# Down products in rounds of three F tiles in a fused attention and GEGLU kernel

## The chip, the cores and the metric

The kernel runs on one core of a Trainium2 chip. The metric is the device time of one execution in microseconds (us); lower is better. TensorE (PE) does the matrix products, VectorE (DVE), ScalarE (ACT) and GpSimd (POOL) the elementwise work, SyncE (SP) issues the DMAs.

## The reference, cut to what matters

Sequence S = 2048, model width D = 576, hidden width F = 4608, H = 32 heads of DH = 18, all in fp32.

```python
def A_ref(x, wqkv, wo):                                   # attention
    q, k, v = split_heads(x @ wqkv)                       # each [H, S, 18]
    p = softmax(einsum("bhqd,bhkd->bhqk", q, k) * 18 ** -0.5)
    return merge_heads(einsum("bhqk,bhkd->bhqd", p, v)) @ wo

def B_ref(x, w_gate, w_up, w_down):                       # GEGLU
    return (gelu(x @ w_gate) * (x @ w_up)) @ w_down

xn = layernorm(x)
return x + A_ref(xn, wqkv, wo) * silu(B_ref(xn, w_gate, w_up, w_down))
```

## The kernel before

**Number format.** Products run on fp32r operands. A factor is split into a high part and a low part, and a product of two factors is made of three matrix products (high·high, high·low, low·high) that accumulate in one PSUM bank. The cut costs two GpSimd instructions a tile (L94 for the high part, L95 for the low part). The names follow it: `wh`, `wl` for gate and up weights, `dh`, `dl` for w_down, `hh`, `hl` for the activated hidden values.

**Prologue (lines 138 to 349).** Layernorm, transpositions and the projections to q, k and v. The split operands of the attention (`qk`, `vs`), the normalised x (`xhs`) and wo go to DRAM and come back by DMA when wanted.

**Sections.** After it the feed-forward part and the attention are interleaved. Tokens are worked in 4 blocks of 512 (`NB`); F is cut into 36 tiles of 128. One *section* works one F tile of one block, so there are 144. In a section TensorE does 27 *pairs* of gate and up products (L369; each pair fills the two halves of the PE rows) into the banks `pg` and `pu`. The first 9 sections (`FIRST`) are the lead, the next 128 carry the attention, the last 7 are the epilogue. The 128 are 32 units (4 heads x 512 queries) of 4 sections (`NA`). In each of them `spread` puts 16 score products (`pe`, L684) and 16 products for the row maxima of a unit to come (`pm`, L653) between the pairs. ScalarE makes the exponentials of `pe` (L685 into `pT`), VectorE the maxima of `pm` (L654).

**End of a section.** What comes behind the pairs stands in this order in the program: the *value block*, 32 products of probabilities and values into `acc` (L718, in column tiles of 32); once in a unit `max_neg` and `max_end` (a transposition of the maxima on TensorE, L667); the `tasks` (output groups, below); `downs` (the down products); and `finish`, in which GpSimd cuts the activated tile `t1` into `hh` and `hl`. The activation itself (`activate`, L382 to L390) runs over ScalarE and VectorE while the next section begins: Square (ScalarE), L383 (VectorE, reads `pg`), a copy of `pg` to `t2` (ScalarE, L386), L387 (VectorE, reads `pu`), Tanh (ScalarE, L388), L390 (VectorE, reads t1 and t2). When a unit ends, ScalarE copies its accumulator to `accs` (L723), a DMA stores that to DRAM (`oT`), and `sums` and `reciprocals` bring the softmax denominators back as `rT`.

**Down products.** Two F tiles (`G` = 2) make a *round*; a block has 18 rounds (`NR`). For a round, `down` makes 8 accumulation groups (4 token tiles x 2 column halves of 288): in each, 3 products a tile, 6 in all (L406), into one of two banks `py` (tag "s", which the scores use as well). VectorE evicts each group into Y, by a copy in the round r == 0 of a block (L410), by an addition otherwise (L412). Within the attention a run has all 8 groups, 48 products, and stands in every second section; around the borders of the attention, and in the last round but one of a block, it is halved into 24 and 24 over two sections:

```python
once = n in ATT and n + G in ATT and r != NR - 2
FF["down"].append((b, r, FF["hs"], wd, FF["Y"], (2 * h, 2 * h + 1), n + 1 + (0 if once else h)))
```

The w_down rows of a round come in one DMA into a tile [128, 2, 576] of the raw buffers (two of them, shared with the raw gate and up weights, which come in as two loads a section and are cut in three pieces of 128x384 each). `hh` and `hl` have 3 buffers each, `dh` and `dl` one.

**Output groups.** When the attention of a block is done, `load_o` brings its sums from DRAM with the reciprocal denominators `den`, `norm_o` multiplies and cuts them on GpSimd (L506), and `project_o` multiplies by wo: 8 groups a block, 15 products each (L550), one in every second section; the group also combines with the gated feed-forward of that block. `gates` (L432) makes the silu of finished Y on ScalarE and GpSimd and stores it. `at(n, part, ...)` files these steps under an attention section.

**Order.** Only TensorE runs in the order that is written in the program; for the other engines a scheduler orders the instructions by their dependencies, save those that are wrapped in `keep_in_program_order`.

**Buffers that the change touches.** VS (values) has 3 buffers (`VB`), `load_v(n + 2)` stands ahead of the value block of section n. KS has 7. `m2` (the negated maxima) has 2, `accs` one of its own, `t2` one.

Of the kernel before, what the change touches and what calls it, by code (L numbers as in the profile page):

```python
# [32 lines left out]
SLOTS = 8  # L33
NA = NS // SLOTS
VC = NT // NA
KB, VB = 7, 3
LEAD = NS + SLOTS
G = 2
NR = F // (G * P)
NF = NB * NR * G  # L40
FIRST = (0, 0, 5, 5, 6, 6, 6, 6, 6)
ATT = range(len(FIRST), len(FIRST) + NU * NA)
MROW = 3 * DH
HO = 7
KO = HO * DH
# [22 lines left out]
def kernel(ctx: ExitStack, tc: tile.TileContext, x, wqkv, wo, w_gate, w_up, w_down, out):  # L68
# [17 lines left out]
    ident = const.tile([P, P], F32, name="ident")  # L86
    make_identity(nc, ident)
    identr = const.tile([P, P], F32R, name="identr")
    nc.gpsimd.tensor_copy(identr, ident)
    all_t = slice(0, TB)  # L90


# [43 lines left out]


    with tc.tile_pool(name="pro", bufs=1) as pro, tc.tile_pool(name="pps", bufs=1, space=PSUM) as pps:

        def load_rest(c0, n):  # L140

# [237 lines left out]
    def activate(pg, pu, early):  # L379

        t1 = ffn.tile([P, TB], F32, name="t1", bufs=1)
        nc.scalar.activation(t1, pg, AF.Square)  # L382
        nc.vector.scalar_tensor_tensor(t1, t1, 1.0 / GC, pg, op0=ALU.add, op1=ALU.mult)  # L383
        if early:
            t2 = ffn.tile([P, TB], F32, name="t2", bufs=1)
            nc.scalar.activation(t2, pg, AF.Copy)  # L386
            nc.vector.tensor_tensor(t2, t2, pu, op=ALU.mult)  # L387
        nc.scalar.activation(t1, t1, AF.Tanh, scale=GC * GS)  # L388
        if early:
            nc.vector.scalar_tensor_tensor(t1, t1, 1.0, t2, op0=ALU.add, op1=ALU.mult)  # L390
        else:
            nc.vector.scalar_tensor_tensor(t1, t1, 1.0, pg, op0=ALU.add, op1=ALU.mult)
            nc.vector.tensor_tensor(t1, t1, pu, op=ALU.mult)
        return t1

    def down(b, r, hs, wd, Y, js):
        for j in js:
            tt = slice(j * P, (j + 1) * P)
            for c in range(2):
                cc = slice(288 * c, 288 * c + 288)  # L400
                py = ps.tile([P, 288], F32, name="py", tag="s", bufs=2)
                n = 0
                for g in range(G):
                    hh, hl = hs[g]
                    for a, w in ((hh, wd[0]), (hh, wd[1]), (hl, wd[0])):
                        nc.tensor.matmul(py, a[:, tt], w[:, g, cc], start=(n == 0), stop=(n == 3 * G - 1))  # L406
                        n += 1
                yy = Y[:, j, cc]
                if r == 0:
                    nc.vector.tensor_copy(yy, py)  # L410
                else:
                    nc.vector.tensor_tensor(yy, py, yy, op=ALU.add)  # L412
                if b == NB - 1 and r == NR - 1:
                    finals.append((Y, j, c))
        if b < NB - 1 and r == NR - 1:
            FF["gates"] += [(b, j, c, Y) for j in js for c in range(2)]

    def gates():
# [17 lines left out]
    def section(specials=(), tag="f", raw_d=None, early=None):  # L436

        n = FF["n"]
        FF["n"] += 1
        b, r = divmod(n // G, NR)  # L440
        g = n % G
# [4 lines left out]
        nxt = load_gu((n + 1) % (NR * G), keep) if n + 1 < NF else None  # L446
        if nxt:
            for k in range(NG - 1):
                split_gu(nxt, k)
        if g == G - 1:  # L450
            raw = FF["rawd"] = raw_d() if raw_d else raw_tile([P, G, D])
            nc.sync.dma_start(raw, w_down[r * G * P:(r + 1) * G * P, :].rearrange("(g p) n -> p g n", p=P))
            if early:
                FF["wd"] = early(raw)
        for p in spread(pairs, specials):
            p()
        if nxt:
            split_gu(nxt, NG - 1)
        FF["w"] = nxt
        if n + 1 < NF and (n + 1) % (NR * G) == 0:  # L460
            FF["xd"] = load_xd(b + 1)
        FF["act"] = activate(pg, pu, n < ATT.stop)

# [6 lines left out]
    def finish(pool=ffn, cut=split, bufs=1):  # L470

        n = FF["n"] - 1
        b, r = divmod(n // G, NR)
        hh = ffn.tile([P, TB], F32R, name="hh", bufs=G + 1)
        hl = ffn.tile([P, TB], F32R, name="hl", bufs=G + 1)
        cut(hh, hl, FF["act"])
        FF["hs"].append((hh, hl))
        if n % G == G - 1:
            wd = FF.pop("wd", None)
            if not wd:  # L480
                wd = [pool.tile([P, G, D], F32R, name=m, bufs=bufs) for m in ("dh", "dl")]
                cut(*wd, FF["rawd"])
            for h in range(2):
                once = n in ATT and n + G in ATT and r != NR - 2
                FF["down"].append((b, r, FF["hs"], wd, FF["Y"], (2 * h, 2 * h + 1), n + 1 + (0 if once else h)))


    op = ctx.enter_context(tc.tile_pool(name="op", bufs=1, reuse_waits="tile"))
# [85 lines left out]
    for b in range(NB):  # L574
        last = b == NB - 1
        for k in range(NK):
            t0 = b * AB + max(-(-min(H, (k + 1) * HO) // QD) * NA + 3, 22 + 3 * k)
            if not (last and k == NK - 1):
                at(t0, 0, load_o, b, k)
                at(t0 + 2 - last, 2, norm_o, k)  # L580
        first = (b + 1) * AB + 1 if last else max((b + 1) * AB + 6, (b + 1) * NR * G - len(FIRST) + 3)
        if not last:
            first += (first + len(FIRST)) % G
        at(first - 2, 0, load_wo, 0)
        at(first - 1, 2, split_o, 0)
        for i in range(GROUPS):
            n = first + i * (1 if last else G)
            if last and n >= ENDS - 1:
                continue
            if not last:  # L590
                at(n, 0, load_xy, b, i)
                at(n + 1, 0, store_y, b, i)
            at(n, 1, lambda b=b, i=i: project_o(b, i, S2[0]))
            if i == TB // P - 1:
                at(n + 1, 0, load_wo, 1)
            if i + 1 < GROUPS:
                at(n, 2, split_o, i + 1)


    with tc.tile_pool(name="att", bufs=1, reuse_waits="tile") as att:  # L600
# [55 lines left out]
        def max_neg(u):  # L656

            nm = att.tile([P, 4 * QD], F32, name="nm", bufs=1)
            nc.vector.tensor_reduce(nm, MX[u].rearrange("p a t c -> p (a t) c"), axis=AX.X, op=ALU.max, negate=True)
            m2 = NM[u] = att.tile([P, 2, 4 * QD], F32R, name="m2", bufs=2)  # L660
            nc.vector.tensor_copy(m2[:, 0], nm)
            nc.vector.tensor_tensor(m2[:, 1], nm, f(m2)[:, 0], op=ALU.subtract)

# [46 lines left out]
        def values(u, kt):  # L710
            j, g = divmod(u, NQ)
            if kt == 0:
                ACC[u] = ps.tile([P, TB], F32, name="acc", tag="acc", bufs=1)
            pt = PT.pop((u, kt))
            for a in range(QD):
                c, t = divmod(kt, VC)
                v = t * VW + (DH + 1) * a
                nc.tensor.matmul(ACC[u][32 * a:32 * a + 32, :], VS[(u * NA + c) % VB][:, v:v + 32], pt[:, a, :],  # L718
                                 start=(kt == 0), stop=(kt == NT - 1), skip_group_check=True)
            if kt == NT - 1:  # L720
                cols = slice(j * TB, (j + 1) * TB)
                acc = att.tile([P, TB], F32, name="accs")
                nc.scalar.activation(acc, ACC[u], AF.Copy)  # L723
                nc.sync.dma_start(oT[g, :, cols], acc)
                rt = rT[QD * g:QD * (g + 1), cols]
                if u < NU - 1:
                    todo.setdefault(((u + 1) * NA, 0), []).insert(0, lambda: sums(u, rt))
                    at((u + 1) * NA + 2, 2, reciprocals, u, rt)
                else:
                    at(NU * NA - 1, 2, last_sums, u, rt)  # L730
# [42 lines left out]
        for n in range(NU * NA):  # L773
# [107 lines left out]
```

## Time and profile before

| | before |
|---|---|
| median of 3 runs, us | 2657.58 |
| lowest, highest, us | 2653.82, 2659.47 |
| profiled execution, us | 2655.82 |
| its span, us | 2654.0 |
| mean granted TensorE clock | 0.999 |
| busy TensorE products / weight loads, us | 2639.6 (99%) / 2052.3 (77%) |
| busy VectorE, us | 2002.5 (75%) |
| busy ScalarE, us | 1504.2 (57%) |
| busy GpSimd, us | 1392.5 (52%) |
| DMA read / written, MB | 266.58 / 52.85 |

The span goes from the first to the last instruction that the profile records, so 1.8 us of the profiled execution lie around it. Busy times are of one profiled execution. A busy TensorE does not say that its products follow each other at the best pace: the ends of products are modelled, and a product that waits in its queue can look long. Distances between the starts of neighbouring products say more. Releasers (`<-`) name the instruction whose end set a waiting one free.

### The profile page before, as it was taken

What the parts mean: (1) busy time and instruction counts of PE and PEld (TensorE: products, weight loads), DVE (VectorE), ACT (ScalarE), POOL (GpSimd) and SP (SyncE); (2) the same over time, 40 slices, a digit from 0 to 9 for tenths busy, and PEclk for the clock granted to TensorE, in tenths of its full rate; (3) what the DMA queues carried; (4) which work ended last, traced back from release to release, by engine and by line L of the source; (5) the groups of instructions that cost most, each with busy time, mean ns of one, the idle gap of its engine ahead of it and who ended that gap; (6) DMA issues with size and microseconds to landing.
All of it is one profiled execution on the core that took longest, in us unless ns stands there. A gap on an engine that the chain in (4) does not pass through costs nothing.

```text
span 2654.0 us, 55993 instructions
## 1 busy us (share of the span) xinstructions
PE 2639.6 (99%) x21032; PEld 2052.3 (77%) x21032; DVE 2002.5 (75%) x3440; ACT 1504.2 (57%) x2690; POOL 1392.5 (52%) x1488
## 2 busy tenths in 40 slices
PE   9999999999999999999999999999999999999999
PEld 8888777777777777777777777777777777777788
DVE  5327888888887888777888887778888877788445
ACT  3222466666666666555666665556666655566632
POOL 2126544545466555555447655554446755555564
PEclk9999999999999999999999999999999999999999
DMA  8875433333345434444336434434335444444341
GB/s 257 265 240 144 115 99 101 98 101 104 98 124 133 106 100 108 121 113 124 100 109 156 117 103 105 124 96 136 104 103 122 133 115 123 107 109 122 77 110 58
DMA packets 390874, 323.66 MB, mean 122 GB/s; under 512 B 105736, under 2 KB 305928, under 8 KB 390604
## 3 DMA queue, kind: packets, MB, share of 16 engines
q1 hardware_dynamic: 390604, 320.08, 44.6%
q8 instruction: 167, 2.74, 0.5%
q14 instruction: 103, 0.84, 0.1%
HBM read 266.58 MB, written 52.85 MB: 120 GB/s over the span
## 4 chain that ended last, share of the span: by engine, by line
PE 97%; POOL 1%; DVE 1%; DMA 1%; issue 0%; ACT 0%; SPq 0%; POOLq 0%; DVEq 0%
PE pg L369 26%; PE py L406 18%; PE acc L718 17%; PE pe L684 10%; PE pm L653 9%; PE pu L369 8%; PE po L159 7%; PE po L550 2%; PE pt L221 0%; POOL wl L95 0%; DVE mx L654 0%; DMA xx<-in_A_x_dram 0%; POOL th L432 0%; PE pm L667 0%; DMA raw<-in_B_w_gate_dram 0%
## 5 line engine op out<-in xcount | busy, mean ns | idle before, releaser
L685 ACT ACTIVATE pT<-pe 128x512 f32<-128x512 f32 x2048 | 1162.8, 599 | 704.1 <-PE pm L653 476.1
L654 DVE TENSOR_REDUCE mx<-pm 128x1 f32<-128x512 f32 x2048 | 1288.5, 685 | 52.1 <-PE pm L653 28.0
L369 PE MATMUL pg<-xd,wh 64*128 64x512 f32 x2592 | 948.3, 398 | 0.5 <-issue 0.5
L369 PE MATMUL pu<-xd,wh 64*128 64x512 f32 x2592 | 948.3, 398 | 0.0
L684 PE MATMUL pe<-q,KS 56*128 56x512 f32 x2048 | 812.5, 405 | 0.0
L653 PE MATMUL pm<-KS,q 54*128 54x512 f32 x2048 | 794.6, 394 | 4.7 <-DVE mx L654 4.7
L369 PEld LDWEIGHTS pg<-xd,wh 64*128 64x128 f32 x2592 | 483.0, 187 | 66.0 <-issue 34.8
L94 POOL TENSOR_SCALAR wh<-raw 128x384 fp32r<-128x384 f32 x432 | 223.8, 519 | 547.6 <-PE pu L369 292.7
L369 PE MATMUL pg<-xd,wl 64*128 64x512 f32 x1296 | 508.2, 392 | 0.0
L369 PE MATMUL pu<-xd,wl 64*128 64x512 f32 x1296 | 507.8, 392 | 0.0
L369 PEld LDWEIGHTS pu<-xd,wh 64*128 64x128 f32 x2592 | 484.1, 187 | 7.6 <-DVE t L387 1.6
L718 PE MATMUL acc<-pT,VS 128*32 128x512 f32 x4096 | 466.0, 595 | 0.0
L95 POOL TENSOR_TENSOR wl<-raw,wh 128x384 fp32r<-128x384 f32 x432 | 442.3, 1025 | 34.3
L684 PEld LDWEIGHTS pe<-q,KS 56*128 56x128 f32 x2048 | 370.2, 184 | 81.3 <-ACT pT L685 20.2
L653 PEld LDWEIGHTS pm<-KS,q 54*128 54x128 f32 x2048 | 377.0, 185 | 29.2 <-DVE mx L654 7.6
L412 DVE TENSOR_TENSOR Y<-py,Y 128x288 f32<-128x288 f32 x544 | 248.7, 457 | 187.6 <-PE py L406 186.7
L406 PE MATMUL py<-dh,hh 128*128 128x288 f32 x1152 | 352.8, 306 | 1.4 <-DVE Y L410 1.2
L406 PE MATMUL py<-dl,hh 128*128 128x288 f32 x1152 | 339.6, 295 | 0.0
L406 PE MATMUL py<-dh,hl 128*128 128x288 f32 x1152 | 338.7, 294 | 0.0
L718 PEld LDWEIGHTS acc<-pT,VS 128*32 128x32 f32 x4096 | 120.6, 109 | 275.7 <-issue 264.4
L369 PEld LDWEIGHTS pg<-xd,wl 64*128 64x128 f32 x1296 | 242.4, 187 | 17.0
L406 PEld LDWEIGHTS py<-dh,hh 128*128 128x128 f32 x1152 | 215.8, 187 | 44.1 <-issue 37.7
(118 smaller groups left out, 2935.2 us busy)
## 6 DMA issues: line engine op xcount, KB each, us to landing
KS<-qk SPq DMA_DIRECT2D x1536, 36.0 KB
raw<-in_B_w_gate_dram SPq DMA_DIRECT2D x144, 288.0 KB
raw<-in_B_w_up_dram SPq DMA_DIRECT2D x144, 288.0 KB
raw<-in_B_w_down_dram SPq DMA_DIRECT2D x68, 576.0 KB
VS<-vs SPq DMA_DIRECT2D x128, 152.0 KB
qk<-t SPq DMA_DIRECT2D x72, 256.0 KB
q<-qk SPq DMA_DIRECT2D x384, 36.0 KB
xd<-xhs SPq DMA_DIRECT2D x24, 384.0 KB
```

The costliest lines, as they stand in the source:

```text
L94: first = nc.gpsimd.tensor_scalar(hi, raw, 1.0, 1.0, op0=ALU.mult, op1=ALU.mult)
L95: nc.gpsimd.tensor_tensor(lo, raw, f(hi), op=ALU.subtract)
L159: nc.tensor.matmul(o, st, m, start=(i == 0), stop=(i == len(TERMS) - 1))
L369: nc.tensor.matmul(o, w[1 + wp][k][rr, c, :], xd[xp][k][rr, c, :], start=(i == 0), stop=(i == len(terms) - 1))
L406: nc.tensor.matmul(py, a[:, tt], w[:, g, cc], start=(n == 0), stop=(n == 3 * G - 1))
L412: nc.vector.tensor_tensor(yy, py, yy, op=ALU.add)
L550: nc.tensor.matmul(po[:, 0:288], o[x][0:n, k, :], OW[w][0:n, k, :], start=(m == 0), stop=(m == len(terms) - 1))
L653: nc.tensor.matmul(pm, QS[u, r][rr, t * P:(t + 1) * P], KS[(u * NA + c) % KB][r][rr, :], start=True, stop=True)
L654: nc.vector.tensor_reduce(MX[u][:, 2 * r + a, t, c:c + 1], pm, axis=AX.X, op=ALU.max)
L684: nc.tensor.matmul(pe, KS[(u * NA + c) % KB][r][rr, t * P:(t + 1) * P], QS[u, r][rr, :], start=True, stop=True)
L685: nc.scalar.activation(PT[u, kt][:, 2 * r + a, :], pe, AF.Exp, scale=SCALE)
L718: nc.tensor.matmul(ACC[u][32 * a:32 * a + 32, :], VS[(u * NA + c) % VB][:, v:v + 32], pt[:, a, :], start=(kt == 0), stop=(kt == NT - 1), s ...
```

## The change

- A round has up to three F tiles (`GM` = 3). The list `ROUNDS` gives the tiles of each round, block by block: block 0 has seven rounds of two, seven of three and one of one; blocks 1 and 2 one of two, eleven of three and one of one; block 3 one of two, eight of three and five of two. `PLACE` maps a section to its block, round, place in the round, size of the round and whether the round is the block's last.
- Within the attention a round's down products stand in one section (`WHOLE`), the one behind its last tile: 8 groups of 9 products, 72, for a round of three; 48 for two; 24 for one. The rounds that are halved are those at the borders of the attention.
- For rounds of three, w_down comes per F tile, [128, 576], a section after the tile's own section (`late`), and is cut into one third of `dh` and `dl`.
- Output groups stand in sections of `WHOLE`, so every third section for the most part, and `load_o` and `norm_o` move (norm_o to one section behind load_o).
- Buffers: `hh` and `hl` keep 3 buffers for 3 tiles in use (3 for 2 before), `dh` and `dl` hold three tiles, VS has 2 and its load is issued behind the value block, `m2` has 1, `accs` shares the buffer of `t2`, and `ident` lives in the prologue's pool only.

The products of the two kernels are the same in number and shape.

```diff
-KB, VB = 7, 3
+KB, VB = 7, 2
-G = 2
-NR = F // (G * P)
-NF = NB * NR * G
+FT = F // P
+NF = NB * FT
+G, GM = 2, 3
+ROUNDS = [[2] * 7 + [3] * 7 + [1], [2] + [3] * 11 + [1], [2] + [3] * 11 + [1], [2] + [3] * 8 + [2] * 5]
+PLACE = [(b, r, g, m, r == len(ms) - 1) for b, ms in enumerate(ROUNDS) for r, m in enumerate(ms) for g in range(m)]
+WHOLE = [n + 1 for n, (b, r, g, m, _) in enumerate(PLACE) if g == m - 1 and n in ATT and n + G in ATT]
...
-            t2 = ffn.tile([P, TB], F32, name="t2", bufs=1)
+            t2 = ffn.tile([P, TB], F32, name="t2")
...
-    def down(b, r, hs, wd, Y, js):
+    def down(b, r, end, hs, wd, Y, js):
...
-                for g in range(G):
-                    hh, hl = hs[g]
+                for g, (hh, hl) in enumerate(hs):
                     for a, w in ((hh, wd[0]), (hh, wd[1]), (hl, wd[0])):
-                        nc.tensor.matmul(py, a[:, tt], w[:, g, cc], start=(n == 0), stop=(n == 3 * G - 1))
+                        nc.tensor.matmul(py, a[:, tt], w[:, g, cc], start=(n == 0), stop=(n == 3 * len(hs) - 1))
...
-        if g == G - 1:
-            raw = FF["rawd"] = raw_d() if raw_d else raw_tile([P, G, D])
-            nc.sync.dma_start(raw, w_down[r * G * P:(r + 1) * G * P, :].rearrange("(g p) n -> p g n", p=P))
+        late = n > 0 and PLACE[n - 1][3] == GM
+        if late:
+            rawd = raw_tile([P, D])
+            nc.sync.dma_start(rawd, w_down[(n - 1) % FT * P:((n - 1) % FT + 1) * P, :])
+        if m < GM and g == m - 1:
+            raw = FF["rawd"] = raw_d() if raw_d else raw_tile([P, m, D])
+            t = n % FT + 1
+            nc.sync.dma_start(raw, w_down[(t - m) * P:t * P, :].rearrange("(g p) n -> p g n", p=P))
...
         for p in spread(pairs, specials):
             p()
+        if late:
+            k = PLACE[n - 1][2]
+            if k == 0:
+                FF["wd3"] = [ffn.tile([P, GM, D], F32R, name=w) for w in ("dh", "dl")]
+            split(*(w[:, k] for w in FF["wd3"]), rawd)
+            if k == GM - 1:
+                FF["down"] = [(*e[:4], FF["wd3"], *e[5:]) if e[4] is None else e for e in FF["down"]]
...
-        hh = ffn.tile([P, TB], F32R, name="hh", bufs=G + 1)
-        hl = ffn.tile([P, TB], F32R, name="hl", bufs=G + 1)
+        hh = ffn.tile([P, TB], F32R, name="hh", bufs=GM)
+        hl = ffn.tile([P, TB], F32R, name="hl", bufs=GM)
...
-                once = n in ATT and n + G in ATT and r != NR - 2
-                FF["down"].append((b, r, FF["hs"], wd, FF["Y"], (2 * h, 2 * h + 1), n + 1 + (0 if once else h)))
+                FF["down"].append((b, r, end, FF["hs"], wd, FF["Y"], (2 * h, 2 * h + 1), n + 1 + (0 if n + 1 in WHOLE else h)))
...
-            t0 = b * AB + max(-(-min(H, (k + 1) * HO) // QD) * NA + 3, 22 + 3 * k)
+            t0 = b * AB + max(-(-min(H, (k + 1) * HO) // QD) * NA + 3, 26 - 2 * last + 2 * k)
...
-                at(t0 + 2 - last, 2, norm_o, k)
-        first = (b + 1) * AB + 1 if last else max((b + 1) * AB + 6, (b + 1) * NR * G - len(FIRST) + 3)
-        if not last:
-            first += (first + len(FIRST)) % G
+                at(t0 + 1, 2, norm_o, k)
+        places = [n - len(FIRST) for n in WHOLE if n - len(FIRST) >= (b + 1) * AB + 5]
+        first = (b + 1) * AB + 1 if last else places[0]
...
-            n = first + i * (1 if last else G)
+            n = first + i if last else places[i]
...
-            m2 = NM[u] = att.tile([P, 2, 4 * QD], F32R, name="m2", bufs=2)
+            m2 = NM[u] = att.tile([P, 2, 4 * QD], F32R, name="m2", bufs=1)
...
-                acc = att.tile([P, TB], F32, name="accs")
+                acc = ffn.tile([P, TB], F32, name="accs", tag="t2")
...
-            load_v(n + 2)
             if i == 1 and u + 2 < NU:
...
                 values(u, kt)
+            load_v(n + 2)
```

More of the change, by code (lines that the diff above doesn't have):

```diff
@@ L84 @@
     xhs = [dram.tile([2, D, TB], F32, name=f"xhs{b}") for b in range(NB)]
-    ident = const.tile([P, P], F32, name="ident")
-    make_identity(nc, ident)
     identr = const.tile([P, P], F32R, name="identr")
-    nc.gpsimd.tensor_copy(identr, ident)
     all_t = slice(0, TB)
@@ L138 @@
     with tc.tile_pool(name="pro", bufs=1) as pro, tc.tile_pool(name="pps", bufs=1, space=PSUM) as pps:
+        ident = pro.tile([P, P], F32, name="ident")
+        make_identity(nc, ident)
+        nc.gpsimd.tensor_copy(identr, ident)
         def load_rest(c0, n):
@@ L412, in down @@
                     nc.vector.tensor_tensor(yy, py, yy, op=ALU.add)
-                if b == NB - 1 and r == NR - 1:
+                if b == NB - 1 and end:
                     finals.append((Y, j, c))
-        if b < NB - 1 and r == NR - 1:
+        if b < NB - 1 and end:
             FF["gates"] += [(b, j, c, Y) for j in js for c in range(2)]
@@ L439, in section @@
         FF["n"] += 1
-        b, r = divmod(n // G, NR)
-        g = n % G
+        b, _, g, m, _ = PLACE[n]
         pairs, pg, pu = gate_up(tag)
@@ L445, in section @@
         keep = tc.keep_in_program_order if n == NU * NA + len(FIRST) + 1 else lambda i: i
-        nxt = load_gu((n + 1) % (NR * G), keep) if n + 1 < NF else None
+        nxt = load_gu((n + 1) % FT, keep) if n + 1 < NF else None
         if nxt:
@@ L459, in section @@
         FF["w"] = nxt
-        if n + 1 < NF and (n + 1) % (NR * G) == 0:
+        if n + 1 < NF and (n + 1) % FT == 0:
             FF["xd"] = load_xd(b + 1)
@@ L472, in finish @@
         n = FF["n"] - 1
-        b, r = divmod(n // G, NR)
-        hh = ffn.tile([P, TB], F32R, name="hh", bufs=G + 1)
-        hl = ffn.tile([P, TB], F32R, name="hl", bufs=G + 1)
+        b, r, g, m, end = PLACE[n]
+        hh = ffn.tile([P, TB], F32R, name="hh", bufs=GM)
+        hl = ffn.tile([P, TB], F32R, name="hl", bufs=GM)
         cut(hh, hl, FF["act"])
         FF["hs"].append((hh, hl))
-        if n % G == G - 1:
+        if g == m - 1:
             wd = FF.pop("wd", None)
-            if not wd:
-                wd = [pool.tile([P, G, D], F32R, name=m, bufs=bufs) for m in ("dh", "dl")]
-                cut(*wd, FF["rawd"])
+            if m < GM and not wd:
+                wd = [pool.tile([P, G if pool is not ffn else GM, D], F32R, name=w, bufs=bufs) for w in ("dh", "dl")]
+                cut(wd[0][:, 0:m], wd[1][:, 0:m], FF["rawd"])
             for h in range(2):
-                once = n in ATT and n + G in ATT and r != NR - 2
-                FF["down"].append((b, r, FF["hs"], wd, FF["Y"], (2 * h, 2 * h + 1), n + 1 + (0 if once else h)))
+                FF["down"].append((b, r, end, FF["hs"], wd, FF["Y"], (2 * h, 2 * h + 1), n + 1 + (0 if n + 1 in WHOLE else h)))
     op = ctx.enter_context(tc.tile_pool(name="op", bufs=1, reuse_waits="tile"))
```

## The prediction

> **What bounds the kernel now.** I read the page first, then the chain of waits in order of time, then the timeline of TensorE, VectorE, ScalarE and GpSimd across single sections.
>
> ```profile
> PE 2639.6 (99%) x21032; PEld 2052.3 (77%) x21032; DVE 2002.5 (75%) x3440; ACT 1504.2 (57%) x2690; POOL 1392.5 (52%) x1488
> ...
> PE 97%; POOL 1%; DVE 1%; DMA 1%; issue 0%; ACT 0%; SPq 0%; POOLq 0%; DVEq 0%
> ```
>
> TensorE is busy for 99% of the span and is 97% of the chain that ends last. The products do not change in number (3456 down products, 21032 in all), so the time can change only through the steps between products. The chain in order of time (start, us, what) shows what a section's end costs:
>
> ```profile
> 361.12 3.57 PE acc L718 x32
> 364.69 6.64 PE py L406 x48
> ...
> 381.71 3.57 PE acc L718 x32
> 385.28 0.43 PE pg L369
> ...
> 416.20 3.57 PE acc L718 x32
> 419.77 0.18 PE pm L667
> ...
> 1021.72 3.57 PE acc L718 x32
> 1025.29 2.18 PE po L550 x15
> 1027.47 6.42 PE py L406 x48
> ```
>
> The value block (L718) takes 3.57 whatever follows it. A run of 48 down products (L406) takes 6.64 behind it, 6.42 behind an output group (L550). A transposition of the maxima (L667) adds 0.18. The timeline shows where a run loses time:
>
> ```profile
> 364.62 0.40 PE L406 MATMUL py<-dh,hh 128*128 128x288 f32 x1
> 364.86 0.30 PE L406 MATMUL py<-dl,hh 128*128 128x288 f32 x1
> 364.99 0.29 PE L406 MATMUL py<-dh,hl 128*128 128x288 f32 x1
> ...
> 366.32 0.31 PE L406 MATMUL py<-dh,hh 128*128 128x288 f32 x1
> 366.47 0.29 PE L406 MATMUL py<-dl,hh 128*128 128x288 f32 x1
> ...
> 371.04 0.29 PE L406 MATMUL py<-dh,hl 128*128 128x288 f32 x1
> 371.26 0.50 PE L369 MATMUL pg<-xd,wh 64*128 64x512 f32 x1
> ```
>
> Averaged over all runs from such starts, one product follows the other by 0.132; 48 of them are 6.35, so 0.29 of the 6.64 is loss. Entry: the second product comes 0.237 after the first (0.24 above), 0.105 too late. Exit: the next pair comes 0.220 after the last product, 0.088 too late. The rest, 0.09, lies in the third to eighth accumulation group, where the bank is used again: the step after the group's first product is 0.15 (366.32 to 366.47), not 0.13. VectorE shows why:
>
> ```profile
> 365.72 0.46 DVE L412 TENSOR_TENSOR Y<-py,Y 128x288 f32<-128x288 f32 x1 [0.84 <-PE py L406]
> ...
> 836.05 1.13 DVE L390 SCALAR_TENSOR_TENSOR t<-t,t 128x512 f32<-128x512 f32 x1
> ```
>
> The first group's last product starts at 365.39; its eviction starts 0.33 later and takes 0.46. The next user of that bank gets going some 0.15 after that, so a bank comes back 0.94 after its group's last start. With six products a group the next user stands there after 7 x 0.132 = 0.93: just too early each time. (The second line is for a rival.)
>
> **The change part by part**, against the profiled execution's 2655.8 us (span 2654.0); the median of the runs is 2657.6, 1.8 above it.
>
> *Fewer runs.* The order of the built program has 63 runs of down products for 83: 37 of 72, 7 of 48 and 19 of 24, where there were 61 of 48 and 22 of 24. Twenty exits go: 20 x 0.088 = -1.8. Runs straight behind a value block fall from 41 to 20: 21 x 0.105 = -2.2. Behind output groups (25 both times) there is no entry loss. Sum -4.0. The page "TensorEngine Tiling (Array Packing)" of the Trainium skill (section Key Properties) says that changing the tiling mode drains TensorE. Taken as one price for every change, with the step from value block to pairs for it (0.52 for 0.10), that makes 20 x 0.42 = -8.4 here; the rows give each change its own price, and I use those.
>
> *Nine products a group.* Where a run holds three F tiles the next user of a bank stands there after 10 x 0.132 = 1.32, the bank is back after 0.94, and the 0.09 a run should vanish. 54 of the 61 runs of 48 go: 54 x 0.09 = -4.9. The other bound is that the 0.015 a group is the price of waiting at all; then only the 17 rounds that no longer exist (72 before, 55 after) save it, -1.5. I take -4.9, because the second group of each run, whose bank was free long before, shows no late step.
>
> *One-tile rounds.* Three blocks end in a round of one tile: 24 products in eight groups of three. There the bank loop of 0.94 stands against 4 x 0.132 = 0.53, so two groups take 0.94 + 2 x 0.132 = 1.21, not 0.79. Following eight groups through, the last product starts 4.39 after the first, not 3.18: +1.2 each, 3.6 in all. Bounds 0 and 5 (VectorE still busy with the activation when the run starts).
>
> *Transpositions.* 28 stand now between value block and pairs (0.18 each); 7 of these will stand before a run or output group, where the average over the three such places is 0.033: -1.0. Pairs behind a transposition alone take 10.15 on average and 10.05 otherwise (8 of 27 wait some 0.37 for L387): -0.7. 27 more sections of pairs follow a value block and not a run, at +0.01: +0.3. Sum -1.4.
>
> *Two stalls.* The first run of blocks 1 and 3 now waits 1.0 and 0.5 for the Y copy (815.8 and 2095.6), because GpSimd, held by a wait for den, cut the activation late. In the built order that GpSimd step (L506) stands a section earlier and there are two sections of cover. -1.0, bounds -1.5 and 0.
>
> *Pieces of w_down, and queues.* 111 pieces at 128x576 replace 55 splits at 128x1152 (1.16 + 2.68). One piece is half of that, 1.92, or the 0.67 + 1.43 of the row of 126x576, 2.10: up to 20 us of GpSimd, which is at 52%. The loads are 56 more issues of 0.4 on SP. Each piece shares the two raw buffers with the gate and up weights: its load waits for their third split, and their next load for its split. Placed by rows (third split from 3.3 into the section, 1.5 long; loads some 3 to 4; piece 1.9; two splits 3.1; hh and hl 1.9), the tightest split ends 15 us before its first product, since weights are cut nearly two sections ahead. Also hh has no spare buffer now: in a section with a run GpSimd waits for the run's end, with the piece and the splits behind it, and they need 5.4 of the 13.9 that the next section lasts. 0. The loads of VS with two buffers wait for the value block of the same section, and are used 24 later: 0.
>
> *ScalarE.* The accumulator's copy (L723, 0.60) takes t2's buffer, so it waits for L390. All 32 copies stand in sections with a run now; 17 will not. There L390 ends 0.26 after the next pairs start (average), the copy lasts to 0.91, and the first exponential starts at 0.92, not 0.83; its bank is wanted 0.3 after its end. 0; up to 17 x 1.0 = +17 if that cover is gone (rival 2).
>
> Sum: -4.0 - 4.9 + 3.6 - 1.4 - 1.0 = -7.7. Execution 2655.8 to 2648.1, median 2657.6 to 2649.9.
>
> **The rivals.** *1: the late step of a reused bank stays.* Then -1.5 stands for -4.9, and the sum is -4.3: 2653.3. For it: the late step has nearly one size everywhere, as a fixed price would. Against it: the loop from the rows (0.94 against 0.93) gives that size too.
>
> *2: ScalarE becomes late.* L390 reads two SBUF tiles. It takes 0.69, but 1.13 at 836.05, where GpSimd's subtraction ran beside it, and 1.53 at most; 16 of 137 are over 0.76. If the new pieces push GpSimd's third or second split under L390, it ends 0.84 later, the copy ends near 1.75, the first exponential is 0.92 late and the third score product waits 0.6. With 16 exponentials of 0.60 in 10.05 us ScalarE cannot catch up, and up to 0.4 returns at the next activation. Seventeen such copies cost 10 to 17: 2660 to 2667. Slower than before it is from 0.45 a copy. Against it: in the order GpSimd's split for the end of the pairs ends 1.8 after them and L390 starts at 3.4; only where GpSimd runs 1.6 late do they meet. The Trainium skill's page "SBUF — State Buffer" (section Who interferes with whom) states the mechanism: a VectorE instruction with two SBUF inputs contends with GpSimd instructions that read SBUF. The trace agrees (0.69 against 1.13), and also in that evictions, with one SBUF input, take 0.46 with GpSimd busy or idle.
>
> *3: every change of tiling costs alike.* With the page's rule -8.4 stands for -4.0: 2645.5. Against it are the rows of entry and exit.
>
> That the change does not do what it says is excluded by the built order (37 runs of 72).
>
> **How the numbers follow.** 0.2% is 5.3 us, about what a measurement of this kernel can tell from no change. Forecast 0.62, rival 1 0.18, rival 2 0.13, rival 3 0.07. The forecast's own range, by the bounds of the one-tile rounds and the stalls, is -10 to -5: 2647 to 2653; 0.06 of it is within 0.2%. Rival 1 (-4.3, +-1) is mostly within: 0.15, and 0.03 faster. Rival 2 gives 0.10 slower and 0.03 within. So faster 0.62 - 0.06 + 0.03 + 0.07 = 0.66, same 0.06 + 0.15 + 0.03 = 0.24, slower 0.10. The range leaves out the worse half of rival 2 and most of rival 3, and takes in run-to-run scatter of the median of 2: 2646 to 2659.
>
> **What would show it.** Right: runs of 72 in the chain at about 9.73 behind a value block (72 x 0.132 + 0.20) and 9.6 behind an output group; steps inside groups all 0.13; three runs of 24 near 4.6; no stall at the first run of a block; TensorE still 97% of the chain. Wrong: a step of 0.15 in each group of nine (rival 1); L390 often over 1.0, exponentials starting later than 1.2 after the pairs' start, waits of pe for ACT (rival 2); any wait of L369 for GpSimd's splits, or of L406 for dl, would say that the cover of the pieces was misjudged.

## The result: slower, and the profile after

| | before | changed |
|---|---|---|
| median, us | 2658.05 (4 runs) | 2674.48 (4 runs) |
| lowest, highest, us | 2653.82, 2659.47 | 2671.98, 2675.79 |
| profiled execution, its span, us | 2655.82, 2654.0 | 2671.98, 2670.2 |
| mean granted TensorE clock | 0.999 | 0.996 |

The ratio is 1.0064, 95% interval 1.0052 to 1.0076: 16 us slower where 7.7 faster was forecast. In the changed kernel the down product is L408, the pairs L372, the value block L729, norm_o's multiplication L518, the activation L385 to L393. The page's busy times and the shares of the chain:

```profile
PE 2641.6 (99%) x21032; PEld 2051.7 (77%) x21032; DVE 1958.0 (73%) x3303; ACT 1502.7 (56%) x2690; POOL 1423.6 (53%) x1602
...
PE 94%; DVE 3%; DMA 1%; POOL 1%; issue 1%; ACT 0%; SPq 0%; POOLq 0%; DVEq 0%; ACTq 0%
```

Busy TensorE moved by 2.0 us and its share of the chain fell from 97% to 94%: products wait, they do not take longer. The chain in order of time (start, us, what) shows runs as forecast, 9.73 behind a value block (forecast 9.73) and 9.51 behind an output group (9.6):

```profile
494.87 3.57 PE acc L729 x32
498.44 9.73 PE py L408 x72
...
1235.13 2.17 PE po L562 x15
1237.31 9.51 PE py L408 x72
```

Elsewhere the chain leaves TensorE. The two largest places, with the pairs at their end:

```profile
1299.97 4.88 DMA OT<-oT
...
1304.98 1.30 POOL OT L518
1306.30 4.78 DMA den<-rT
...
1312.46 0.62 POOL hh L94
...
1313.16 1.29 POOL hl L95
...
1314.47 0.60 ACT t L385
...
1317.19 0.50 PE pu L372
```

```profile
1374.19 9.28 DMA raw<-in_B_w_down_dram
...
1383.54 0.67 POOL dh L94
...
1388.83 0.59 POOL hh L94
...
1389.49 1.27 POOL hl L95
...
1390.79 0.60 ACT t L385
...
1392.88 0.76 PE pg L372
```

Read them from the end. The pairs wait for a bank that the activation has not read. Its Square (L385) waits for t1, whose last reader is the cut `hl` of the tile before. That cut stands on GpSimd behind an instruction that waits for a DMA: norm_o for OT and den in the first, a piece of w_down in the second, whose load was issued among those of q, OT and wo and took 9.28 us. TensorE stood 1.9 and 5.2 us. (Its waits put the first down to the cut `dl`, which ended at the same moment, 1316.56; the pairs do not read it. The copy of `pg`, L389, ended at 1316.42 and freed the bank.) The windows show what came on top (columns: window, length, busy PE, PEld, DVE, ACT, POOL, granted clock, DMA share, GB/s):

```profile
1387.70:1390.00 2.30, 0.00 (x0) 0.00 (x0) 0.00 (x0) 0.00 (x0) 2.13 (x4) 1.00 1.10 250
1390.00:1392.50 2.50, 0.00 (x0) 0.00 (x0) 0.69 (x1) 0.96 (x2) 2.23 (x3) 0.57 0.39 111
1393.50:1396.50 3.00, 3.00 (x15) 2.40 (x16) 2.08 (x3) 1.05 (x2) 0.15 (x1) 0.50 0.62 167
1397.50:1400.50 3.00, 3.00 (x30) 2.63 (x28) 3.00 (x6) 2.34 (x6) 2.92 (x4) 1.00 0.29 74
...
1319.00:1322.00 3.00, 3.00 (x16) 2.43 (x16) 2.15 (x5) 1.92 (x4) 0.00 (x0) 0.50 1.10 244
```

The clock is at 0.50 for 3.4 and 4.3 us of the pairs that follow: 15 or 16 products in 3 us, then 30. The pairs behind the two stalls are 2.1 and 2.2 us longer than usual, most of it by that.

By the starts of products, section by section (the usual length of each kind of section end and of the pairs times its count, and what exceeds it), the 16.2 us between the spans are:

| | us | forecast |
|---|---|---|
| section ends: fewer runs, nine products a group, transpositions before runs | -9.8 | -9.9 |
| three one-tile rounds (from the last product of the pairs to the next pairs 8.52, not 7.29) | +3.7 | +3.6 |
| usual length of the pairs, 123 full sections | +1.6 | -0.4 |
| prologue and end | -1.5 | 0 |
| stalls and late activations above that | +22.2 | -1.0 |

The stalls: GpSimd's late cuts 4.0 at 1314, 7.5 at 1387 and 3.2 at 1467, late KS loads 5.8 (1334, 1934, 2149), ScalarE 0.9 (849), the rest small.

### The profile page after: what moved, and what is told of

It is laid out like the page before. It is cut to its first block, busy times and chain, and to the rows that moved or that the text cites. A ratio compares the mean times of both kernels' runs of the same rounds, so it can differ in the third digit from the quotient of the medians.

```text
span 2670.2 us, 56169 instructions
## 1 busy us (share of the span) xinstructions
PE 2641.6 (99%) x21032; PEld 2051.7 (77%) x21032; DVE 1958.0 (73%) x3303; ACT 1502.7 (56%) x2690; POOL 1423.6 (53%) x1602
## 4 chain that ended last, share of the span: by engine, by line
PE 94%; DVE 3%; DMA 1%; POOL 1%; issue 1%; ACT 0%; SPq 0%; POOLq 0%; DVEq 0%; ACTq 0%
PE pg L372 25%; PE py L408 17%; PE acc L729 16%; PE pe L695 10%; PE pm L664 8%; PE pu L372 8%; PE po L162 7%; PE po L562 2%; DVE mx L665 1%; DMA raw<-in_B_w_down_dram 0%; PE pt L224 0%; DVE Y L414 0%; DVE t L386 0%; DVE t L390 0%; POOL wl L95 0%
## 5 line engine op out<-in xcount | busy, mean ns | idle before, releaser
L372 PE MATMUL pg<-xd,wh 64*128 64x512 f32 x2592 | 951.2, 399 | 8.1 <-ACT t L389 5.6
L372 PE MATMUL pu<-xd,wh 64*128 64x512 f32 x2592 | 950.4, 399 | 0.6 <-DVE t L390 0.5
L372 PEld LDWEIGHTS pg<-xd,wh 64*128 64x128 f32 x2592 | 484.5, 187 | 92.9 <-issue 34.1
L372 PE MATMUL pu<-xd,wl 64*128 64x512 f32 x1296 | 509.2, 393 | 0.0
L372 PE MATMUL pg<-xd,wl 64*128 64x512 f32 x1296 | 509.0, 393 | 0.0
L372 PEld LDWEIGHTS pu<-xd,wh 64*128 64x128 f32 x2592 | 485.7, 187 | 8.6 <-DVE t L390 2.9
L729 PE MATMUL acc<-pT,VS 128*32 128x512 f32 x4096 | 466.0, 595 | 0.0
L414 DVE TENSOR_TENSOR Y<-py,Y 128x288 f32<-128x288 f32 x408 | 185.3, 456 | 235.9 <-PE py L408 235.0
L408 PE MATMUL py<-dh,hh 128*128 128x288 f32 x1152 | 346.4, 301 | 4.4 <-DVE Y L412 2.7
L94 POOL TENSOR_SCALAR wh<-raw 128x384 fp32r<-128x384 f32 x432 | 233.8, 542 | 214.6 <-PE pu L372 102.9
L408 PE MATMUL py<-dh,hl 128*128 128x288 f32 x1152 | 339.8, 295 | 0.0
L408 PE MATMUL py<-dl,hh 128*128 128x288 f32 x1152 | 338.9, 294 | 0.0
L729 PEld LDWEIGHTS acc<-pT,VS 128*32 128x32 f32 x4096 | 120.2, 109 | 276.6 <-issue 261.6
L94 POOL TENSOR_SCALAR dh<-raw 128x576 fp32r<-128x576 f32 (+1 forms) x121 | 86.5, 715 | 404.1 <-DMA raw<-in_B_w_down_dram 390.8
L372 PEld LDWEIGHTS pg<-xd,wl 64*128 64x128 f32 x1296 | 242.9, 187 | 16.6
```

The source lines that it names most:

```text
L94: first = nc.gpsimd.tensor_scalar(hi, raw, 1.0, 1.0, op0=ALU.mult, op1=ALU.mult)
L372: nc.tensor.matmul(o, w[1 + wp][k][rr, c, :], xd[xp][k][rr, c, :], start=(i == 0), stop=(i == len(terms) - 1))
```

## The experiments

Each is named by what it changes; the kernel before ran on the same chip.

**Does the slowness come with the buffers, the pieces or the output part?** First the changed kernel with rounds of two only:

```diff
-ROUNDS = [[2] * 7 + [3] * 7 + [1], [2] + [3] * 11 + [1], [2] + [3] * 11 + [1], [2] + [3] * 8 + [2] * 5]
+ROUNDS = [[2] * 18] * 4
```

> The changed kernel with eighteen rounds of two F tiles in every block: no pieces of w_down, no run of 72, output groups every second section again; all the buffer changes stay (two VS buffers with the load behind the value block, one m2, the accumulator's copy in t2's buffer, no more than three hh and hl, norm_o one section behind load_o). Theory A (the pieces of w_down, through the two shared raw buffers and the in-order queues of GpSimd and SP, cause the stalls): about the time before, 2655 to 2661 us. Theory B (output groups every third section push the next block's OT loads together behind the last cut of OT, and GpSimd is held there): the same, 2655 to 2661. Theory C (the smaller buffers cause the stalls): 2666 us or more, with waits of the pairs for the activation and of the maxima for KS.

2677.95 us (ratio 1.008, 1.0065 to 1.0095). No theory had this. The time went in three places, 8.3, 7.7 and 6.6 us over the usual length of the pairs, each where a block begins: TensorE waits for GpSimd's copy of the reloaded xd. The split of w_down waits for the end of the run, the raw buffer and with it the gate load wait for the split, and xd stands behind that load on SP (issued from 757.8 on, before from 751.5 on). The kernel before halves the last round but one there; `WHOLE` does not know it. With the halving restored:

```diff
-n + 1 + (0 if n + 1 in WHOLE else h)
+n + 1 + (0 if n + 1 in WHOLE and r != 16 else h)
```

> The changed kernel with rounds of two in every block, and the last round but one of a block halved over two sections as in the kernel before, so that the reload of xd at the border of blocks isn't held up (what cost the other run with rounds of two some 22 us). Buffers, VS load behind the value block, load_o places as changed; norm_o not pinned. Theory B: output groups are at every second section, nothing bunches: 2654 to 2662 us. Theory C (the smaller buffers cost by themselves): 2666 us or more.

2656.65 us (0.9998, 0.9988 to 1.0008). Smaller VS, m2, the shared buffer of accs and the moved loads cost nothing: theory C falls, and the 21 us of the run before were the border.

**The pieces alone**, first added to the run with the trouble at the border (w_down of sections 14 to 133, save the first round of a block, a section late, by F tile), then to the one with the halving restored, here without a block's last two rounds as well:

```diff
-        late = n > 0 and PLACE[n - 1][3] == GM
+        late = n > 0 and n - 1 in PIECES      # PIECES: the sections named above
```

> As the run with rounds of two, but w_down of sections 14 to 133 (save the first round of a block) comes in pieces of one F tile, a section late, through the shared raw buffers, as in the changed kernel. Runs stay at 48, output groups at every second section. Theory A: 5 to 15 us over the run with rounds of two, with the piece's first split waiting for its DMA (over 300 us in all), KS loads issued late and waits of the pairs for ScalarE's Square behind hl. Theory B: within 3 us of the run with rounds of two.

2683.30 us, 5.3 over the run without pieces.

> The run with rounds of two and a halved last round but one (2656.7), with w_down of the middle rounds of each block in pieces of one F tile, a section late, through the shared raw buffers. Output groups at every second section, a spare hh and hl. Prediction's step (pieces cost 0): 2655 to 2659 us. Theory A (pieces alone cost, as the 5.3 us between the two earlier runs with rounds of two say): 2660 to 2664 us, mostly as waits of pu for VectorE's L390 in sections behind a transposition.

2666.32 us (1.0032, 1.0020 to 1.0044), 9.7 over the run without pieces. So the pieces are not free. The trace has no stall over 1 us but 19 of 27 sections behind a transposition alone in which the pairs are over 0.15 us longer than usual (8.4 us in all; 2 of 27 and 1.2 us without pieces). VectorE in such a place, of before and of the changed kernel:

```profile
486.27 0.34 DVE L661 CAST m<-nm 128x16 fp32r<-128x16 f32 x1
486.64 0.17 DVE L662 TENSOR_TENSOR m<-nm,m 128x16 fp32r<-128x16 f32 x1
486.74 0.68 DVE L383 SCALAR_TENSOR_TENSOR t<-t,pg 128x512 f32<-128x512 f32 x1
```

```profile
481.04 0.90 DVE L672 CAST m<-nm 128x16 fp32r<-128x16 f32 x1
481.98 0.43 DVE L673 TENSOR_TENSOR m<-nm,m 128x16 fp32r<-128x16 f32 x1
482.33 0.67 DVE L386 SCALAR_TENSOR_TENSOR t<-t,pg 128x512 f32<-128x512 f32 x1
```

The cast of max_neg takes 0.175 with GpSimd idle. Beside a GpSimd instruction it takes 0.59 and 0.60 on average in the run with pieces and in the changed kernel, 0.26 and 0.39 in the kernel before and in the run without pieces; over 0.6 it took 14 and 13 times of 32, against once and twice. The pieces push GpSimd's cuts to the end of the pairs, where max_neg runs, and the activation behind it comes late. That is read from the traces; no run moves max_neg or the cuts alone. The Trainium skill's page "SBUF — State Buffer" (section Who interferes with whom) names casts among the VectorE instructions that can contend with GpSimd for the pair of ports that both use; the trace agrees (0.175 against 0.59).

**A raw buffer for the pieces**, paid for with one buffer less for wh and wl:

```diff
-            rawd = raw_tile([P, D])
+            rawd = wts.tile([P, D], F32, name="rawd")
...
-        hi, lo = (wts.tile([P, XG, P], F32R, name=m, bufs=5) for m in ("wh", "wl"))
+        hi, lo = (wts.tile([P, XG, P], F32R, name=m, bufs=4) for m in ("wh", "wl"))
```

> The changed kernel with a raw buffer of its own for the pieces of w_down, so that gate and up weights have the two raw buffers to themselves in the rounds of three; to make room wh and wl have four buffers each, not five. Theory A: the KS stalls (5.8 us by the changed kernel's trace) and the stall behind the piece that landed late (7.5) go, the stall behind norm_o (4.0) and the one behind the gates (3.2) stay: 2655 to 2666 us. Theory B: 2670 to 2676 us, as the changed kernel.

2671.18 us (1.0053, 1.0038 to 1.0068). The stalls of the changed kernel moved to other places: waits for KS (4.0 us) and for the cuts of wh and wl (4.8) took over. With two changes in it, it settles nothing on theory A.

**norm_o in its place.** The scheduler had moved norm_o's multiplication ahead of its place in the program, by three sections where the first stall is:

```diff
-        nc.gpsimd.tensor_tensor(OT[0:n, k, :], OT[0:n, k, :], den[0:n], op=ALU.mult)
+        tc.keep_in_program_order(nc.gpsimd.tensor_tensor(OT[0:n, k, :], OT[0:n, k, :], den[0:n], op=ALU.mult))
```

> The changed kernel with the multiplication of norm_o pinned behind what precedes it on GpSimd in the program, so that the scheduler no longer moves it ahead by several sections to stand and wait for den. Theory A: only the stall at 1314 us goes, 4 us: 2668 to 2672 us. Theory B: that one and those that follow from GpSimd running late around the border of blocks 1 and 2 (1387, 1467) go, 10 to 15 us: 2659 to 2665 us.

2653.46 us, 10 runs (0.9985, 0.9976 to 0.9995): 21 us less than the changed kernel, below the ranges of both theories, and some 4 us faster than before. The orders of VectorE and ScalarE are the same in both programs; only GpSimd's and SP's differ. GpSimd by its timeline, at the place of the first stall, pinned:

```profile
1292.80 0.81 POOL L565 TENSOR_TENSOR yy<-yy,xx 128x288 f32<-128x288 f32 x1
1299.19 0.62 POOL L94 TENSOR_SCALAR hh<-t 128x512 fp32r<-128x512 f32 x1 [5.58 <-PE py L408]
1299.89 1.30 POOL L95 TENSOR_TENSOR hl<-t,hh 128x512 fp32r<-128x512 f32 x1
```

and changed:

```profile
1293.53 0.81 POOL L565 TENSOR_TENSOR yy<-yy,xx 128x288 f32<-128x288 f32 x1
1304.98 1.29 POOL L518 TENSOR_TENSOR OT<-OT,den 126x512 f32<-126x512 f32 x1 [10.64 <-DMA OT<-oT]
1311.21 1.28 POOL L518 TENSOR_TENSOR OT<-OT,den 126x512 f32<-126x512 f32 x1 [4.94 <-DMA den<-rT]
1312.46 0.62 POOL L94 TENSOR_SCALAR hh<-t 128x512 fp32r<-128x512 f32 x1
```

The cut of hh follows the run's end by itself in the one (its buffer has no spare), and comes some 13 us later in the other. GpSimd's waits of L518 for DMAs were 101 us in the changed kernel, 6 in the pinned one. In the kernel before they were 99 us (L506) with no more lost than two stalls of 1.1 and 0.6 us: what counts is what stands behind them. The same pin in the kernel before:

> The kernel before with the one pin of norm_o's multiplication behind what precedes it on GpSimd in the program. Theory B (what slows the change is norm_o, moved ahead by the scheduler and held for den, because the longer output phase bunches the loads of OT): the pin takes away only the two stalls of before (1.0 and 0.5 us), 2654 to 2658 us. Rival D (the pin is a gain of its own, whatever the change, by another order of GpSimd and SP): 10 to 20 us faster than before, 2637 to 2648 us.

2655.55 us (0.9999, 0.9989 to 1.0008): the pin is no gain of its own (rival D falls).

**What makes norm_o's hold hurt?** The output part alone in the kernel before (the first part of block 3's OT is loaded ahead of block 2's last cut, so block 2's last group mixes two blocks):

```diff
-            t0 = b * AB + max(-(-min(H, (k + 1) * HO) // QD) * NA + 3, 22 + 3 * k)
+            t0 = b * AB + max(-(-min(H, (k + 1) * HO) // QD) * NA + 3, 26 - 2 * last + 2 * k)
...
-                at(t0 + 2 - last, 2, norm_o, k)
+                at(t0 + 1, 2, norm_o, k)
...
-            n = first + i * (1 if last else G)
+            n = first + i * (1 if last else 3)
```

> The kernel before with the output part of the change alone: output groups in every third section, load_o and norm_o at the changed places; rounds of two, all buffers and w_down as before. Theory B: the three OT loads of the next block bunch behind the last cut of OT, GpSimd is held for them and for den, with stalls as in the changed kernel: 4 to 16 us slower, 2661 to 2674 us. Rival A (it takes the pieces of w_down as well): within 3 us of before, 2654 to 2661 us.

2656.94 us (1.0000, 0.9991 to 1.0010). Theory B fails as it was put. The three OT loads bunch here too (1315 to 1318) and norm_o waits, but GpSimd's timeline has the cut of hh ahead of it, and only the split of w_down behind:

```profile
1310.76 0.62 POOL L94 TENSOR_SCALAR hh<-t 128x512 fp32r<-128x512 f32 x1 [2.15 <-DVE t L390]
...
1320.04 1.29 POOL L506 TENSOR_TENSOR OT<-OT,den 126x512 f32<-126x512 f32 x1 [4.19 <-DMA OT<-oT]
...
1326.72 1.29 POOL L506 TENSOR_TENSOR OT<-OT,den 126x512 f32<-126x512 f32 x1 [4.26 <-DMA den<-rT]
1327.97 2.67 POOL L95 TENSOR_TENSOR dl<-raw,dh 128x1152 fp32r<-128x1152 f32 x1
```

One stall stands in this trace all the same, at the first run of block 2 (2.1 us at 1455, with the half clock behind it 3.9; none there before): hh is cut behind the gates, and these behind a norm_o that waited 5.5 us for den. The stalls of before, 1.1 and 0.6 us, are gone, so the time hardly shows it.

With `bufs=G` for hh and hl (no spare) and the groups starting at `(b + 1) * AB + 5`:

> The kernel before with output groups at every third section from the fifth of a block, load_o and norm_o as changed, and hh and hl without a spare buffer (two for rounds of two); w_down not in pieces. The earlier run had the output part alone and was as fast as before, though its OT loads bunched and norm_o held GpSimd as in the changed kernel. Theory E (the hold hurts only where hh has no spare, since the cut of the next round's first tile has to wait for the run and so stands behind norm_o): stalls of the pairs behind late cuts, 4 to 15 us slower than before, 2660 to 2672 us. Theory F (the hold hurts only together with the pieces of w_down, which share the raw buffers and GpSimd's and SP's order): within 3 us of before, 2653 to 2660 us.

2734.85 us (1.0283, 1.0266 to 1.0300). Nearly all of it lies at halved runs: there both buffers stay taken for two sections, Square starts 9.5 to 14.5 us late at four places, and the epilogue loses some 13. At whole runs nothing is lost, and at the bunched loads hh stands ahead of norm_o. Neither theory E nor F is told apart by it; what it shows is why the changed kernel, with no spare, needs whole runs. Pieces with the long output phase, hh with its spare (`n = first + 3 * i` for the groups):

> As the run before this one, with output groups at every third section from the first possible one, so that the next block's OT loads bunch behind the last cut; hh and hl keep their spare. Theory F: 4 to 15 us over the run with pieces alone, by stalls behind norm_o, late pieces and late KS loads in the stretch behind the last output group of a block. Theory E: within 3 us of the run with pieces alone.

2665.95 us, within 1 us of the pieces alone, though its trace has the stall at block 2's first run too (2.4 us at 1463): theory F falls for rounds of two.

**Is the late cut the link?** hh and hl of the attention's sections cut by ScalarE and VectorE:

```diff
-        cut(hh, hl, FF["act"])
+        (split_av if cut is split else cut)(hh, hl, FF["act"])
```

> The changed kernel, norm_o not pinned, with hh and hl cut by ScalarE (high part) and VectorE (low part) in the attention's sections, not by GpSimd. Theory G (TensorE stalls because the cut of hh and hl stands in GpSimd's queue behind an instruction that waits for a DMA, and the single t1 hands that to the next activation): the stalls of the pairs behind hl (16 us with the half clock after them, in the trace of the changed kernel) go, 2655 to 2663 us, if the two engines take 128 more instructions of 0.6 and 0.7 us each at no cost. If it is KS, the weights or the bank of Y that is late first, the time stays over 2668 us.

> As the run before this one, with norm_o pinned as well. Theory G: the pin has little left to take away, within 4 us of the run before this one. If norm_o held TensorE by another way than hh and hl (KS loads behind den in SP's queue, weights behind it on GpSimd): 8 us or more faster than it.

> Control: the kernel before with hh and hl cut by ScalarE and VectorE. What the move costs by itself, where GpSimd made no stall but two (1.0 and 0.5 us): 2655 to 2663 us; more than that would have to be taken off the two other runs.

2724.87, with the pin 2722.92, the control 2713.70 us (1.0218, 1.0201 to 1.0235). The move itself costs 57 us, which no expectation had: in the first of the three pm waits 16.9 us for VectorE's maxima, py 8.1 for its evictions, pe 6.7 for ScalarE. Within that the test holds: unpinned, norm_o waits for DMAs as long as in the changed kernel (99 us), yet in the attention Square starts at most 0.51 us after the last gate product's end (usually 0.36) where it was up to 6.75, and the pin is worth 2 us where it was worth 21. So norm_o reached TensorE by way of the cut of hh and hl. The caution is that another engine sets the pace in these three.

**The one-tile rounds.** Pinned, without them (here too the first part of block 3's OT is loaded ahead of block 2's last cut):

```diff
+ROUNDS = [[2] * 6 + [3] * 8, [3] * 12, [3] * 12, [3] * 8 + [2] * 6]
```

> The changed kernel with norm_o pinned and without rounds of one tile: six of two and eight of three in block 0, twelve of three in blocks 1 and 2, eight of three and six of two in block 3. By the terms: three runs of 24 less (3 x 1.2 of waiting for banks, 3 entries and exits of 0.2) against the pinned kernel's 2653.5: 2647 to 2651 us. Rival (the one-tile round covers the reload of xd at the border of blocks, as the halved round did before): TensorE waits there for GpSimd's copy of xd, 5 to 8 us at each of three borders: 2662 to 2676 us.

2674.36 us (1.0068, 1.0053 to 1.0083): the rival. The pairs lose 8.0, 9.2 and 7.4 us at the borders. By the waits of TensorE (total, times, longest):

```profile
PE pu L372 <- POOL xd L129: 15.5, 13, 2.6
```

The one-tile round that costs 1.2 us a block covers a reload worth 8. Ends in rounds of two, the last but one halved (`[2] * 7 + [3] * 6 + [2] * 2`, `[3] * 10 + [2] * 3` twice):

> The changed kernel with norm_o pinned, and blocks 0 to 2 ending in rounds of two with the last but one halved over two sections (as before covers the reload of xd) where the changed kernel has a one-tile round: seven of two, six of three, two of two; ten of three and three of two twice; block 3 as changed. By the terms 0.8 us less a block (the bank waits of a run of 24 with groups of three go, an exit, an entry and the late steps of two rounds of two come): 2650 to 2653 us. If the halved round does not cover the reload where w_down comes in pieces: 5 us or more at a border, 2658 us or more.

2664.78 us (1.0030, 1.0019 to 1.0041). xd is covered, but behind two borders GpSimd is late again, now with the gates and a late up load ahead of hl (5.8 and 2.9 us, and 2.0 and 2.2 more in the pairs that follow, with half the clock):

```profile
1442.68 6.93 DMA raw<-in_B_w_up_dram
...
1458.89 1.54 POOL th L434 x2
1460.43 0.59 POOL hh L94
...
1461.10 1.27 POOL hl L95
```

So norm_o is one occupant of the queue, not the only one. Last, the one-tile rounds kept, their groups over five banks:

```diff
+                one = len(hs) == 1 and (2 * j + c) % 5 > 1
+                py = ps.tile([P, TB], F32, name="py", tag="m", bufs=3)[:, 0:288] if one else ...  # as it was
```

> The changed kernel with norm_o pinned, and the eight groups of a one-tile round spread over five banks (two of the scores', three of the maxima's) where they had two. If the 1.2 us that such a run loses is the wait for its bank, three such runs give back up to 3.6 us: runs of 24 at 3.3 to 3.6 us where they took 4.6, and 2650 to 2652 us against 2653.5 for the pinned kernel. If it is VectorE that is late there (eight evictions of 0.46 behind the activation), less than 1 us comes back.

2650.62 us, 12 runs (0.9983, 0.9975 to 0.9992), the lowest median of all; against the kernel before its interval overlaps the pinned kernel's, so the gain in time is not shown. The three runs of down products, first to last start, take 3.16 to 3.17 where they took 4.41 to 4.66. So it was the two banks, not VectorE, that made them long.

## Why the prediction was wrong, step by step

*Fewer runs and nine products a group: right.* Section ends gave -9.8 with the transpositions before runs. A step from a run to pairs is 0.220 as before, a group's second step in a reused bank is 0.126 to 0.134 on average in runs of 72 (before, in runs of 48, 0.138 to 0.154). Rivals 1 and 3 fall.

*One-tile rounds: right in size,* and by the reason given; not seen was what they are for.

*Pieces of w_down, and queues: 0. This is the step that failed:* the stalls came to 22.2 us, and the pin of one GpSimd instruction took 21 off the time. The place by rows asked when the weights are needed, and they never were late. It also noted that hh has no spare and that the piece and the splits stand behind its wait, 5.4 of 13.9 us. What it left out stands in the same queue: norm_o with two DMA waits (18 us from 1294 to 1312), the gates, a piece whose DMA took 9.3; and behind them hl, t1 and the next Square. It named L369's wait for splits as the sign of a misjudged cover; the sign was L385's wait for hl. Pieces by themselves also cost some 10 us on rounds of two, by the traces through max_neg.

*Two stalls: -1.0. Failed with it.* "GpSimd step (L506) stands a section earlier" was read as cover. Earlier on GpSimd meant ahead of the cut of hh, waiting for loads that bunch behind the previous block's last cut.

*Rival 2 had the engine pair right and, but for one case, the place wrong.* L393 took over 1.0 in 35 sections of 137 (before 9), but only once did it cost TensorE time by way of the accumulator's copy, 0.9 us (timelines of VectorE and ScalarE):

```profile
847.85 1.75 DVE L393 SCALAR_TENSOR_TENSOR t<-t,t 128x512 f32<-128x512 f32 x1
```

```profile
849.69 0.60 ACT L734 ACTIVATE accs<-acc 128x512 f32<-128x512 f32 x1 [2.15 <-DVE t L393]
```

*The range* had no rival for a held GpSimd queue, and no price for the clock after a stall. Without the missed step the sum was nearer: pinned, the time is 3.8 below before by the medians (forecast -7.7, the forecast's own range -10 to -5); by the spans it is 5.4 (2648.6), but that execution is the fastest of the pinned kernel's ten.

Open: the late KS loads (5.8 us) went with the pin, and SP's queue then differs as well; that norm_o caused them was not tried alone. Why the scheduler set norm_o ahead of hh in the changed kernel and not in the one without a spare is inferred from the buffer's wait, not shown.

## What to carry to other kernels

On an engine that works in order, ask of each instruction that can wait for a DMA what stands behind it and who is released by that, not only when its own result is needed; here a multiplication with several sections of slack held a cut that had none. Where a scheduler orders an engine, pin what waits for DMA behind the work that feeds the bound engine. An odd small round or a halved run at a border may be cover: find what reloads there before counting it as waste.

## What the hardware showed unasked

TensorE's granted clock fell to 0.50 after stalls of 1.9 (1314), 2.1 (1934) and 5.2 us (1387): from 1318.7 to 1322.1, from 1936.5 to 1939.9 and from 1390.4 to 1397.2. The products behind took 2.1, 1.7 and 2.2 us longer, in the first case in part because `pu` still waited for L390. It did not fall after a stall of 2.7 us in a run of down products (1467; 1.00 in the windows on both sides). That is not a matter of the kind of product: stalls of 2.1 us at 1455 (the output part alone) and 2.4 us at 1463 (pieces and the long output phase), both in such runs, brought half the clock from 1458.7 and 1466.0 on. In every trace here the clock falls only at whole multiples of 3.41 us from one fall to the next, and the stall at 1467 lies across such a border (1468.9); whether that spared it is not shown. The Trainium skill's page "TensorE: Matmul & The Clock Gate" (section What's actually happening) states half the clock after at least one idle window of about 3.4 us; here stalls of 1.9 and 2.1 us, shorter than that, sufficed.
